# r's stationary operand at 64 columns, u's operands at 64 rows, and the tokens' split issued behind the move of r, in a chunked attention kernel with two MLPs

## The chip, the cores and the metric

The kernel runs on one core of one Trainium2 chip. The metric is the device time in microseconds (us) of one execution. TensorE (PE in the rows; PEld are its weight loads), VectorE (DVE), ScalarE (ACT), GpSimd (POOL) and SyncE (SP, which issues the DMAs) each work through a list of instructions of their own, in the order in which it was written into the program.

## What is computed

Three layers, all in float32. The first is a recurrence over 768 tokens, for 4 batches and 8 heads of width 40; the other two are a SiLU MLP (320 to 2048 and back) and a gated MLP (320 to 1536 and back) over the 3072 rows that come out of it.

```python
for t in range(S):                       # S = 768, state is [B, H, 40, 40]
    y[:, :, t] = einsum('bhd,bhde->bhe', r_t, state)
    Sa = einsum('bhde,bhe->bhd', state, a_t)
    state = state * w_t[:, :, None, :] - outer(Sa, b_t) + outer(v_t, k_t)
x = silu(y_rows @ w_in) @ w_out
x = (sigmoid(x @ w_gate) * (x @ w_val)) @ w_out2
```

## The kernel before

**The recurrence.** The tokens are cut into 24 chunks of C = 32. A unit is one chunk of one batch, and n counts the units, 0 to 95, four batches to a chunk. Inside a unit the 32 tokens are solved at once: a triangular system is inverted on VectorE ahead of time (`z`, `zh`, `zs`), and the unit itself is a row of small float32 matmuls over its 8 heads, each head written as a pair (i, g) with i in 0..1 and g in 0..3. Of a pair of heads one writes the PSUM partitions from 0 on and the other those from 64 on. In the profile each of these matmuls appears as two instructions, a transpose as one. The groups of a unit, by the names of their PSUM tiles:

- `ps_r` (`c_rhs`, L472): the right side of the system, 96 rows deep, from the tokens' tile `xt` (stationary, 32 columns a head) and the state's tile `sr`. ScalarE moves the result to the tile `rb` in two copies (L476). This move of r is what the title speaks of.
- `ps_u` (`c_u`, L486): the inverse, `zs`, times `rb`, 32 rows deep. ScalarE writes the result into `sr` (L488).
- `ps_ut` (L520), `ps_t` (L513), `wt` (L447): transposes. ScalarE moves `wt` to `ks` and `yl` (L450, L451).
- `ps_y` (L543) and `ps_s` (L498): output and new state, both 128 rows deep with 40 columns of weights. VectorE takes them to `stg` (L551) and `sr` (L503).
- `ps_lp` (L529): 64 rows deep, 32 columns of weights, 32 instructions. VectorE takes it to `yr` (L532).
- `lb` (L258): for units that are prepared ahead, 64 rows deep and 64 columns of weights.

All of these but some of the `lb` share one pool of four PSUM buffers (`pt`).

**The order on TensorE.** A loop over n writes the groups out by a string of letters. For n under 16 it is `cuRqz0tp1vys23l`, and the digits are warming matmuls (`acc_w`) that compute nothing. From n = 16 on it is `zcqu0123vtpRysl`; the digits are now a share of the first MLP: 16 matmuls `hp` (L608) and 12 matmuls `acc` (L630 to L632). From there each step reads `ps_lp`, `ps_u`, `hp`, `acc`, `ps_ut`, `ps_t`, `wt`, `ps_r` of the next unit, `ps_y`, `ps_s`. After n = 95 the first MLP goes on alone to n = 111, and then comes the gated MLP.

**Work issued behind other work.** A dictionary `last_q` keeps the last instruction of a unit on ScalarE ("a") and on VectorE ("v"). `behind()` has what is written inside it come after these two in the engines' lists. Three users: the split of the tokens (`x_split`, L589 to L592), which every eighth step makes high and low parts of the recurrence's output for the first MLP; the conversions of the first MLP's weights (`wtick`); and those of the gated MLP's weights (`conv2`). Before the change `last_q["a"]` is the copy of `wt` to `yl` in `prep` (L451), which stands ahead of the move of r on ScalarE. The tool that builds the kernel settles the rest of each engine's order with a timeline of its own, and gives out the PSUM buffers by it.

**Setup.** `setup2` zeroes with ScalarE the parts of the tiles that no DMA fills.

Of the kernel before, what the change touches and what calls it, by code (L numbers as in the profile page):

```python
# [8 lines left out]
F32 = mybir.dt.float32  # L9
# [9 lines left out]
H, D, C, NB = 8, 40, 32, 4  # L19
# [3 lines left out]
KO, WO, EW = 4 * C, 12 * C, 12 * C + GW  # L23
# [10 lines left out]
def kernel(  # L34
# [71 lines left out]
    vu = cp.tile([64, 8, H, C], F32, name="vu")  # L106
    zf = vu[:].rearrange("p a h c -> p (a h c)")[:, 5 * H * C:].rearrange("p (x h c) -> p x h c", x=2, h=H)

    zs2 = [cp.tile([96, 2, 4, C], F32, name=f"zs{i}") for i in range(2)]
    rb = [cp.tile([96, 4, D], F32, name=f"rb{i}") for i in range(2)]  # L110

    etb = [cp.tile([ER, 2, EW], F32, name=f"et{i}") for i in range(NEB)]
    wib = [cp.tile([ER, 2, GW], F32, name=f"wi{i}") for i in range(2)]
# [36 lines left out]
    def setup2(units):  # L150

        for k in units:
            zero(sr[k][32:64])
            if k < 3:
                zero(yl[k][0:64])
            if k < 1:
                zero(ks[k][0:64])
                nc.scalar.copy(ks[k][0:D], ident[0:D, 0:D].unsqueeze(1).to_broadcast([D, H, D]))
            if k < NB:
                zero(sr[k][0:D])  # L160
            if k < NCB:
                zero(yr[k][32:64])
            if k < NXB:
                zero(xt_l(k, 32, 64))
            if k == 0:
                flat = lambda t: t.rearrange("p b h c -> p (b h c)")
                zero(flat(vr2))
                zero(flat(vu[32:64, 0:5]))
                zero(zf)
# [256 lines left out]
            nc.scalar.copy(zs2[n // 2 % 2][64 * i:64 * i + B2, :, :, B2:], ps[:, :, 4 - 4 * i:8 - 4 * i])  # L426

    def xt_a(k, h):
        i, g = divmod(h, 4)
        return xt[k][:, 1 - i, C * g:C * (g + 1)]  # L430

    def xt_l(k, p0, p1):
        return xt[k][p0:p1, :, 0:KO]

    def xt_w(k):
        w = xt[k][0:D, 1, WO:EW].rearrange("p (g s) -> p g s", s=W33)
# [30 lines left out]
    def c_rhs(n):  # L467
        k, s = n % NCB, n % NSB
        ps = pt.tile([128, 4, D], F32, tag="pt", name="ps_r")
        for g in range(4):  # L470
            for i in range(2):
                last_pe[0] = nc.tensor.matmul(  # L472
                    ps[64 * i:64 * i + C, g], xt_a(n % NXB, 4 * i + g), sr[s][0:96, 4 * i + g, :], start=True, stop=True
                )
        for i in range(2):
            nc.scalar.copy(rb[n % 2][64 * i:64 * i + C], ps[64 * i:64 * i + C])  # L476
        rhs_i[n] = last_op[0] = last_pe[0]

    def c_u(n):
# [2 lines left out]
        ps = pt.tile([128, 4, D], F32, tag="pt", name="ps_u")  # L482
        for g in range(4):
            for i in range(2):
                x = slice(64 * i, 64 * i + C)
                last_op[0] = nc.tensor.matmul(ps[x, g], z[x, g], r[x, g], start=True, stop=True)  # L486
        for i in range(2):
            nc.scalar.mul(sr[s][96:128, 4 * i:4 * i + 4], ps[64 * i:64 * i + C], -1.0)  # L488

# [812 lines left out]
```

## Time and profile before

| | us |
|---|---|
| median of 3 runs | 1331.74 |
| lowest, highest run | 1330.07, 1333.38 |
| the profiled execution, its own time | 1330.02 |
| its span, first to last instruction | 1328.3 |
| TensorE busy in the span | 1253.2 (94%) |
| TensorE weight loads busy | 1144.0 (86%) |
| VectorE busy | 762.2 (57%) |
| ScalarE busy | 609.3 (46%) |
| mean granted TensorE clock | 0.972 of 2.4 GHz |

The stages of the span, read from the rows of TensorE: setup to about 54 us, units n = 1 to 15 with warming matmuls to about 215, units 16 to 95 with the first MLP to about 838, the rest of the first MLP to about 911, and the gated MLP to the end. The times of one row are those of one profiled execution. A start of a group minus the start of the group before it is what the earlier group costs the engine, a change between the two included; a matmul's own duration is longer than that, since matmuls overlap.

### The profile page before, as it was taken

The page shows a single profiled execution, that of the slowest core. Times are in us where ns is not written, and L with a number is a line of the kernel's source. Part 1 is how long each engine was busy: PE and PEld are TensorE (multiplying, and loading weights), DVE is VectorE, ACT ScalarE, POOL GpSimd, SP SyncE. Part 2 cuts the span into 40 slices and gives each one's busy share as a digit, 9 for nine tenths or more (in the row PEclk, how much of TensorE's full clock was granted, in tenths as well). Part 3 has the DMA queues.
Part 4 walks back from the last instruction along what each step waited for, and adds up shares of the span by engine and source line. Part 5 has one row for each costly group of instructions (what it writes and reads, how often), then busy time and mean ns, then how long its engine had stood idle before and what let it go on. Part 6 is the DMA issues. An engine that isn't in the chain of part 4 may idle for free. (4 is left out here: it accounts for less than half of the span.)

```text
span 1328.3 us, 44838 instructions
## 1 busy us (share of the span) xinstructions
PE 1253.2 (94%) x18785; PEld 1144.0 (86%) x18785; DVE 762.2 (57%) x2014; ACT 609.3 (46%) x1498; POOL 207.8 (16%) x303
## 2 busy tenths in 40 slices
PE   3788989899999999999999999999999999999996
PEld 3688888899999999989999999988888888888885
DVE  7356775868686777767685733477952323232322
ACT  4236555555555555545555555577532222222221
POOL 3124445311111111111110000133310000000000
PEclk9888887899999999999999999999999999999998
DMA  7666656454545455545544231345610101000000
GB/s 187 143 147 160 187 155 168 138 131 130 130 122 151 117 148 121 142 118 139 133 129 103 70 92 42 91 121 191 186 52 5 35 6 34 7 12 8 12 10 23
DMA packets 167557, 135.98 MB, mean 102 GB/s; under 512 B 89538, under 2 KB 129858, under 8 KB 167346
## 3 DMA queue, kind: packets, MB, share of 16 engines
q1 hardware_dynamic: 167346, 133.02, 38.5%
q8 instruction: 151, 2.47, 0.8%
q14 instruction: 60, 0.49, 0.1%
HBM read 95.15 MB, written 37.48 MB: 100 GB/s over the span
## 5 line engine op out<-in xcount | busy, mean ns | idle before, releaser
L608 PE MATMUL hp<-X,w 120*128 120x256 f32 x1536 | 212.1, 292 | 1.4 <-issue 1.4
L608 PEld LDWEIGHTS hp<-X,w 120*128 120x128 f32 x1536 | 193.9, 194 | 5.7 <-issue 1.5
L1077 DVE TENSOR_TENSOR sg<-hv,sg 128x512 f32<-128x512 f32 x72 | 49.7, 690 | 186.2 <-PE hv L1069 161.5
L1069 PE MATMUL hg<-XT,wgv 128*128 128x512 f32 x576 | 151.2, 394 | 0.5 <-ACT x L639 0.5
L1069 PE MATMUL hv<-XT,wgv 128*128 128x512 f32 x576 | 147.2, 394 | 0.0
L1069 PEld LDWEIGHTS hv<-XT,wgv 128*128 128x128 f32 x576 | 107.3, 188 | 23.5
L1069 PEld LDWEIGHTS hg<-XT,wgv 128*128 128x128 f32 x576 | 105.9, 188 | 21.4 <-ACT x L639 0.8
L630 PE MATMUL acc<-o1h,gh 128*128 128x320 f32 x384 | 119.9, 312 | 2.2 <-ACT gh L618 2.2
L632 PE MATMUL acc<-o1h,gl 128*128 128x320 f32 x384 | 119.4, 311 | 1.8 <-DVE gl L619 1.8
L619 DVE TENSOR_TENSOR gl<-hp,gh 128x512 fp32r<-128x512 f32 x96 | 65.9, 687 | 92.9 <-ACT gh L618 92.6
L631 PE MATMUL acc<-o1l,gh 128*128 128x320 f32 x384 | 119.0, 310 | 0.0
L674 POOL TENSOR_TENSOR cvt<-cvt,cvr 128x256 int32<-128x256 int32 (+3 forms) x85 | 73.3, 868 | 283.4 <-DVE cvt L673 201.6
L551 DVE TENSOR_TENSOR stg<-ps_y,xt 40x128 f32<-40x128 f32 x192 | 55.0, 287 | 105.6 <-PE ps_y L543 102.5
L488 ACT ACTIVATE sr<-ps_u 32x160 f32<-32x160 f32 x192 | 56.4, 294 | 120.0 <-PE ps_u L486 117.8
L617 ACT ACTIVATE hp<-hp 128x512 f32<-128x512 f32 x96 | 55.9, 582 | 121.1 <-PE hp L608 121.1
L341 DVE TENSOR_TENSOR ztmp<-zh,z 128x126 f32<-128x126 f32 (+22 forms) x310 | 97.0, 313 | 7.8 <-DMA z<-sN 1.4
L345 DVE TENSOR_TENSOR zh<-zh,ztmp 128x126 f32<-128x126 f32 (+22 forms) x310 | 97.9, 316 | 6.0
L1078 ACT CAST gh<-sg 128x512 fp32r<-128x512 f32 x72 | 44.6, 620 | 123.6 <-DVE sg L1077 123.4
L1076 ACT ACTIVATE sg<-hg 128x512 f32<-128x512 f32 x72 | 42.9, 596 | 121.6 <-PE hg L1069 121.6
L462 PE MATMUL acc_w<-identr 128*128 128x256 f32 x536 | 87.4, 330 | 1.1 <-issue 1.1
L1089 PE MATMUL a<-o,gh 128*128 128x320 f32 x288 | 87.9, 309 | 0.0
L1088 PE MATMUL a<-o,gh 128*128 128x320 f32 x288 | 87.6, 310 | 0.3 <-ACT gh L1078 0.3
(147 smaller groups left out, 2408.2 us busy)
## 6 DMA issues: line engine op xcount, KB each, us to landing
xt<-sE SPq DMA_DIRECT2D x48, 322.5 KB
sE<-et SPq DMA_DIRECT2D x84, 161.2 KB
et<-in_wkab_dram SPq DMA_DIRECT2D x80, 161.2 KB
cvr<-in_moe_w_out_dram SPq DMA_DIRECT2D x28, 320.0 KB
X<-sX SPq DMA_DIRECT2D x144, 40.0 KB
z<-sN SPq DMA_DIRECT2D x20, 256.0 KB
cvr<-in_moe_w_in_dram SPq DMA_DIRECT2D x42, 100.0 KB
sr<-in_vn_dram SPq DMA_DIRECT2D x48, 80.0 KB
```

Of the source, the lines that this page charges most:

```text
L341: nc.vector.tensor_tensor(tv, z[:, 0:rows, s:s + 1].to_broadcast([128, rows, m]), nt[:, s:s + 1, s + 1:].to_broadcast([128, rows, m]), op= ...
L345: last_inv[0] = nc.vector.tensor_tensor(z[:, 0:rows, s + 1:], z[:, 0:rows, s + 1:], tv, op=ALU.add)
L462: last_op[0] = nc.tensor.matmul(ps[:, :128 * w], identr, identr.unsqueeze(1).to_broadcast([128, w, 128]), start=True, stop=True,)
L608: last_op[0] = nc.tensor.matmul(hp[:, half, :], w1[0:rows, wi_, f * 128:(f + 1) * 128], X[xi][0:rows], start=(pi == 0), stop=(pi == 7),)
L619: nc.vector.tensor_tensor(gl, hp, gh.bitcast(F32), op=ALU.subtract)
L630: nc.tensor.matmul(acc_t[c], a, o1(0, f), start=(f == 0), stop=False)
L631: nc.tensor.matmul(acc_t[c], a, o1(1, f), start=False, stop=False)
L632: last_op[0] = nc.tensor.matmul(acc_t[c], gl[:, fi, 128 * c:128 * c + 128], o1(0, f), start=False, stop=(f == NF1 - 1))
L674: nc.gpsimd.tensor_tensor(ti, ti, lo, op=ALU.add)
L1069: nc.tensor.matmul(hp, wgv[mi][f // 4][0:rows, wi_, f % 4 * 128:f % 4 * 128 + 128], X[0:rows, xi, :], start=(pi == 0), stop=(pi == 7))
L1088: nc.tensor.matmul(acc2_t[t], a, o2[0][f], start=(f == 0), stop=False)
L1089: nc.tensor.matmul(acc2_t[t], a, o2[1][f], start=False, stop=False)
```

## The change

Three edits. (1) `xt_a` hands `ps_r` 64 columns of weights for each head in place of 32, and the matmul writes 64 PSUM partitions in place of 32; the upper 32 are not read. The columns that are read beyond the old ones must be finite, so `setup2` zeroes a further part of `xt`. (2) `rb` and `zs` have 128 partitions in place of 96, their rows 32 to 63 and 96 to 127 are zeroed in setup, and `ps_u` is 64 rows deep in place of 32. (3) `last_q["a"]` is set to the move of r as well, so that whatever `behind()` issues in units from 16 on stands behind it. In units under 16 `prep` is written after `c_rhs` and sets `last_q["a"]` again.

```diff
-    zs2 = [cp.tile([96, 2, 4, C], F32, name=f"zs{i}") for i in range(2)]
-    rb = [cp.tile([96, 4, D], F32, name=f"rb{i}") for i in range(2)]
+    zs2 = [cp.tile([128, 2, 4, C], F32, name=f"zs{i}") for i in range(2)]
+    rb = [cp.tile([128, 4, D], F32, name=f"rb{i}") for i in range(2)]
...
                 zero(xt_l(k, 32, 64))
+                zero(xt_l(k, 64, 96))
+            if k < 2:
+                for p in (32, 96):
+                    zero(rb[k][p:p + 32])
+                    zero(zs2[k][p:p + 32].rearrange("p x g c -> p (x g c)"))
...
     def xt_a(k, h):
         i, g = divmod(h, 4)
-        return xt[k][:, 1 - i, C * g:C * (g + 1)]
+        return xt[k][:, 1 - i, C * g:C * (g + 2)]
 
     def xt_l(k, p0, p1):
-        return xt[k][p0:p1, :, 0:KO]
+        return xt[k][p0:p1, :, (KO if p0 == 64 else 0):KO + C]
...
                 last_pe[0] = nc.tensor.matmul(
-                    ps[64 * i:64 * i + C, g], xt_a(n % NXB, 4 * i + g), sr[s][0:96, 4 * i + g, :], start=True, stop=True
+                    ps[64 * i:64 * i + 64, g], xt_a(n % NXB, 4 * i + g), sr[s][0:96, 4 * i + g, :], start=True, stop=True
                 )
         for i in range(2):
-            nc.scalar.copy(rb[n % 2][64 * i:64 * i + C], ps[64 * i:64 * i + C])
+            last_q["a"] = nc.scalar.copy(rb[n % 2][64 * i:64 * i + C], ps[64 * i:64 * i + C])
...
-                x = slice(64 * i, 64 * i + C)
-                last_op[0] = nc.tensor.matmul(ps[x, g], z[x, g], r[x, g], start=True, stop=True)
+                x = slice(64 * i, 64 * i + 64)
+                last_op[0] = nc.tensor.matmul(ps[64 * i:64 * i + C, g], z[x, g], r[x, g], start=True, stop=True)
```

ScalarE in a step with a split (one of those at n = 23, 31, ... 87 and 95), from the copies of `wt` on; `X` is the tile of the first MLP's input. Before:

```order
L450 COPY ks_188<-wt 64x320
L451 COPY yl_186<-wt 64x320
L589 CAST X<-X 120x512
L590 CAST X<-X 120x256
L476 COPY rb_175<-ps_r 32x160 x2
L488 ACTIVATE sr_184<-ps_u 32x160 x2
L617 ACTIVATE hp<-hp 128x512
```

After:

```order
L456 COPY ks_188<-wt 64x320
L457 COPY yl_186<-wt 64x320
L482 COPY rb_175<-ps_r 32x160 x2
L595 CAST X<-X 120x512
L596 CAST X<-X 120x256
L494 ACTIVATE sr_184<-ps_u 32x160 x2
L623 ACTIVATE hp<-hp 128x512
```

The two casts have moved from ahead of the two copies to `rb` to behind them; nothing else has moved there.

ScalarE in step n = 19, while weights of the first MLP are still being converted (`cvt`, `cvr`, `w`, `o1h` are tiles of that conversion). Before:

```order
L450 COPY ks_188<-wt 64x320
L451 COPY yl_185<-wt 64x320
L670 ACTIVATE cvt<-cvr 128x320
L671 ACTIVATE cvr<-cvr 128x320
L694 CAST w_158<-cvt 120x128 x2
L476 COPY rb_175<-ps_r 32x160 x2
L488 ACTIVATE sr_182<-ps_u 32x160 x2
L703 CAST o1h_3840<-cvt 128x320
```

After:

```order
L456 COPY ks_188<-wt 64x320
L457 COPY yl_185<-wt 64x320
L482 COPY rb_175<-ps_r 32x160 x2
L676 ACTIVATE cvt<-cvr 128x320
L677 ACTIVATE cvr<-cvr 128x320
L700 CAST w_158<-cvt 120x128 x2
L494 ACTIVATE sr_182<-ps_u 32x160 x2
L709 CAST o1h_3854<-cvt 128x320
```

The copies to `rb` have moved ahead of four instructions of the conversion. Steps 17 and 18 show the same exchange.

TensorE at the same place, from `ps_r` to the first matmuls of the first MLP, with the engines that each row waits for. Before:

```order
L472 MATMUL ps_r<-sr_182,xt_165 32x40 [waits PE_49]
L543 MATMUL ps_y<-yr_168,yl_187 40x32 [waits Activation_49]
L498 MATMUL ps_s<-sr_182,ks_188 40x40 [waits Activation_49]
L529 MATMUL ps_lp<-yr_169,vu 32x32 [waits DMAHW2_49,DMAHW4_49,PE_49,Activation_49]
L486 MATMUL ps_u<-rb_175,zs_173 32x40 [waits DVE_49,PE_49,Activation_49]
L486 MATMUL ps_u<-rb_175,zs_173 32x40 [waits Activation_49]
L608 MATMUL hp<-X,w_158 128x256 x16
```

After:

```order
L478 MATMUL ps_r<-sr_182,xt_165 64x40 [waits PE_49]
L549 MATMUL ps_y<-yr_168,yl_187 40x32 [waits Activation_49]
L504 MATMUL ps_s<-sr_182,ks_188 40x40 [waits Activation_49]
L535 MATMUL ps_lp<-yr_169,vu 32x32 [waits DMAHW2_49,DMAHW5_49,PE_49,Activation_49]
L492 MATMUL ps_u<-rb_175,zs_173 32x40 [waits PE_49,Activation_49]
L614 MATMUL hp<-X,w_158 128x256 x16
```

The groups stand in the same order. `ps_r` is 64 wide, and `ps_u` no longer waits for VectorE, since with `rb` copied earlier it is given the PSUM buffer that `ps_r` leaves and not that of `ps_y`. In the steps that hold an `lb` (even n from 20 to 78) `ps_u` waits for VectorE before and after the change alike; at n = 18, which holds one too, it does so only after.

## Rows read from the trace of the kernel before

**Rows 1.** Busy us by stage: stretch, length, engines, granted clock, DMA share, GB/s.

```profile
54.00:215.00 161.00, 145.40 (x2983) 135.28 (x2985) 100.71 (x283) 80.96 (x227) 62.76 (x80) 0.87 0.62 159
262.00:838.00 576.00, 569.98 (x12137) 529.97 (x12134) 387.53 (x1164) 305.64 (x796) 65.06 (x111) 1.00 0.47 117
```

**Rows 2.** Timeline of TensorE, one step without a split: start, us, group, count.

```profile
502.84 0.48 PE L472 MATMUL ps_r<-sr,xt 96*32 96x40 f32 x16
503.25 0.50 PE L543 MATMUL ps_y<-yr,yl 128*40 128x32 f32 x16
503.58 0.50 PE L498 MATMUL ps_s<-sr,ks 128*40 128x40 f32 x16
504.01 0.70 PE L529 MATMUL ps_lp<-yr,vu 64*32 64x32 f32 x32
504.64 0.48 PE L486 MATMUL ps_u<-rb,zs 32*32 32x40 f32 x16
505.04 2.17 PE L608 MATMUL hp<-X,w 120*128 120x256 f32 x16
```

**Rows 3.** Timeline of TensorE, the next step, where an lb stands.

```profile
511.09 1.12 PE L258 MATMUL lb<-et 64*64 64x32 f32 x32
512.14 0.70 PE L529 MATMUL ps_lp<-yr,vu 64*32 64x32 f32 x32
```

**Rows 4.** Weight loads by line: count, busy us, mean ns, idle before.

```profile
L258 PEld LDWEIGHTS lb<-et 64*64 64x64 f32 x1344 | 44.0, 139 | 11.9 <-DVE et L235 9.2
L486 PEld LDWEIGHTS ps_u<-rb,zs 32*32 32x32 f32 x1536 | 36.4, 108 | 15.4 <-ACT rb L476 8.2 <-issue 2.9
L472 PEld LDWEIGHTS ps_r<-sr,xt 96*32 96x32 f32 x1536 | 34.7, 113 | 4.9
```

**Rows 5.** Waits of TensorE from 262 us on: total us, times, longest.

```profile
PE ps_u L486 <- ACT rb L476: 3.6, 10, 0.7
```

**Rows 6.** Timeline of TensorE in a step with a split, n = 55.

```profile
534.46 0.69 PE L529 MATMUL ps_lp<-yr,vu 64*32 64x32 f32 x32
535.47 0.78 PE L486 MATMUL ps_u<-rb,zs 32*32 32x40 f32 x16 [0.32 <-ACT rb L476]
536.18 2.06 PE L608 MATMUL hp<-X,w 120*128 120x256 f32 x15
```

**Rows 7.** Timeline of ScalarE in the same step.

```profile
534.31 0.62 ACT L589 CAST X<-X 120x512 fp32r<-120x512 f32 x1
534.84 0.40 ACT L590 CAST X<-X 120x256 fp32r<-120x256 f32 x1
535.14 0.58 ACT L476 COPY rb<-ps_r 32x160 f32<-32x160 f32 x2
```

**Rows 8.** Timeline of TensorE in steps 17 and 19.

```profile
234.25 0.70 PE L529 MATMUL ps_lp<-yr,vu 64*32 64x32 f32 x32
235.79 0.78 PE L486 MATMUL ps_u<-rb,zs 32*32 32x40 f32 x16 [0.84 <-ACT rb L476]
...
252.20 0.70 PE L529 MATMUL ps_lp<-yr,vu 64*32 64x32 f32 x32
255.12 0.74 PE L486 MATMUL ps_u<-rb,zs 32*32 32x40 f32 x16 [2.23 <-DVE stg L551]
```

**Rows 9.** Busy us in stretches around these steps, columns as in Rows 1.

```profile
236.80:240.10 3.30, 3.30 (x17) 3.30 (x16) 3.13 (x11) 1.16 (x4) 2.18 (x3) 0.50 0.83 240
240.30:253.70 13.40, 12.59 (x296) 11.56 (x294) 11.06 (x35) 9.40 (x28) 3.63 (x6) 1.00 0.53 151
253.90:260.60 6.70, 5.48 (x37) 5.42 (x38) 6.34 (x18) 2.00 (x5) 2.27 (x3) 0.50 0.55 160
```

**Rows 10.** Timeline of TensorE, u of the last unit.

```profile
836.42 0.78 PE L486 MATMUL ps_u<-rb,zs 32*32 32x40 f32 x16 [0.65 <-ACT rb L476]
```

**Rows 11.** ScalarE at the end of setup, and one of its zeroing groups.

```profile
42.17 0.42 ACT L450 COPY ks<-wt 64x320 f32<-64x320 f32 x1 [26.67 <-PE wt L447]
...
L148 ACT ACTIVATE xt<-ident 32x256 f32<-32x256 f32 x6 | 2.4, 404 | 0.0
```

## The prediction

> **What bounds the kernel now.** I read the busy time by stage first. From 262 to 838 us TensorE is busy 569.98 of 576 us at full granted clock, while VectorE is busy 387.53 and ScalarE 305.64 of them [rows 1]. There the order of TensorE's groups is the path: what a group costs the engine is the next start minus its own, and a microsecond taken out of the row comes off the end, since the rest of the first MLP follows on the same engine and the gated MLP's weights are converted behind the last unit of the recurrence. From 54 to 215 us TensorE is busy 145.40 of 161 us, at a mean clock of 0.87, and VectorE and the DMAs hold it up in places [rows 1]; there a change of TensorE's work counts only in part. Then I read one step in order of time [rows 2, 3], the waits that are left in it [rows 5], and the steps in which they fall [rows 6 to 8, 10].
>
> **A change of shape between groups.** `ps_y` and `ps_s` have the same shape of weights and 16 instructions each. From `ps_y` to `ps_s` it takes 503.58 - 503.25 = 0.33 us, from `ps_s` to `ps_lp`, whose weights have another shape, 504.01 - 503.58 = 0.43 [rows 2]. I take 0.10 us as the price of a change of shape. It can be less, since `ps_s` also streams 40 columns and `ps_y` 32: I let it lie between 0.05 and 0.13. The change removes two of these in each step from n = 16 on: from `ps_r` to `ps_y` and from `ps_lp` to `ps_u`. Those before `ps_r` and behind `ps_u` stay, since `wt` and `hp` have other shapes still.
>
> **The wider loads of r.** `ps_r` to `ps_y` takes 503.25 - 502.84 = 0.41 us with a change, so 0.31 without, 19 ns for each of 16 instructions of 32 columns of weights [rows 2]. The trace has 64-column loads in `lb`: 512.14 - 511.09 = 1.05 us with a change behind it, 0.95 without, for 32 instructions [rows 3], so 0.475 for 16. `ps_r` to `ps_y` becomes 0.475 in place of 0.41: +0.065, the change of shape already taken off.
>
> The row of weight loads gives 139 ns for a load of 64 columns and 113 ns for one of 32 [rows 4]; these durations overlap, since a pair for two halves of PSUM runs side by side, and the starts above are what the engine pays. The Trainium skill (TensorE: Matmul & The Clock Gate, "LDWEIGHTS (loading the stationary operand)") has a load take its columns divided by 1.2, in ns, whatever its rows. By that 32 columns more would cost 26.7 ns for each load, an estimate of 0.43 us for 16, and the sum would be nearly that of rival 1. The starts of `lb` disagree.
>
> I go by the starts: 0.475 - 0.31 = 0.165 us for the loads of one `ps_r`.
>
> **The deeper operands of u.** Loads of 32 columns take 108 ns at 32 rows and 113 ns at 96 [rows 4], so 64 rows cost u nothing of note. `ps_lp` to `ps_u` is 504.64 - 504.01 = 0.63 us; without the change of shape 0.53. That is -0.10.
>
> A step gives +0.065 - 0.10 = -0.035 us, and 80 steps (n = 16 to 95) -2.8. With c for the price of a change of shape the step is 0.115 - 1.5 c, so 80 steps give +3.2 at c = 0.05 and -6.4 at 0.13.
>
> **The tokens' split.** Ten times `ps_u` waits for the copies to `rb`, 3.6 us in all [rows 5]. At n = 55 it starts 535.47 - 534.46 = 1.01 us behind `ps_lp` in place of 0.63, and `hp` starts 0.71 behind it in place of 0.40, since its second matmul waits for the second copy [rows 2, 6]. That is 0.38 + 0.31 = 0.69 us. The copies stand behind two casts of the split, which begin at 534.31 [rows 7]. With the casts behind them the copies run from 534.31 to 534.89; `ps_u` would start at 534.46 + 0.065 + 0.53 = 535.05, and the wait is gone with about 0.16 us to spare. What comes late next: the casts run until about 535.7, and the move of u to `sr` behind them. The first MLP's matmuls cover that (`hp` alone lasts 2.17 us [rows 2]) until `ps_ut` reads u, and the split's result is read a step later. Nine steps give 9 x 0.69 = -6.2. The tenth is n = 95, where the idle time is 0.65 and not 0.32 [rows 10], but where fewer groups stand between `ps_r` and `ps_u`; I take -0.8, between -0.3 and -1.1.
>
> **The conversions of the first MLP's weights.** In steps 17 and 19 `ps_u` starts 235.79 - 234.25 = 1.54 and 255.12 - 252.20 = 2.92 us behind `ps_lp` [rows 8], 0.91 and 2.29 more than in a plain step: 3.2 us. The first wait is for `rb`, behind the conversions on ScalarE, which now stand behind it. The second is for VectorE's `stg`, because `ps_u` had been given the buffer that `ps_y` leaves; it no longer is. After both waits the granted clock is 0.50 (1.2 of 2.4 GHz) for 3.3 and for 6.7 us [rows 9]. If it stays up, half of 3.3 and some 2.4 more come back, 4.0 in all. Against that stands VectorE: from 236.8 to 260.6 it is idle for only 0.17 + 2.34 + 0.36 = 2.9 us [rows 9], and `ps_u` of steps 18 and 20 waits for its `stg`. TensorE can gain the 0.9 of step 17 and then about 2.9 before VectorE stops it: 3.8. I take -3.5, with 0 and -7.2 as ends.
>
> **Units 1 to 15.** There the neighbours of `ps_r` are `ps_u` and `ps_lp`, both of other shapes before and after, so nothing is saved, and `ps_r` grows by 0.475 + 0.10 - 0.41 = 0.165 us: 15 x 0.165 = +2.5 if every bit lies on the path, 0 if the 15.6 us in which TensorE idles there [rows 1] take it up. I take +1.2. The order of some DMAs on SP moves there too; I have no row for what that does, and let it be within 2 us either way.
>
> **Setup.** ScalarE gets 14 more zeroing instructions, six more of which have grown. The nearest row has 0.404 us for 256 elements, so at most 5.7 us. ScalarE then waits 26.67 us for TensorE at 42.17 [rows 11], which covers it: 0.
>
> **Sum.** -2.8 - 6.2 - 0.8 - 3.5 + 1.2 = -12.1 us. The profiled execution took 1330.02 us by its own time (span 1328.3), which makes 1317.9; it lies 1.7 below the median of the runs shown, 1331.74, so the median to expect is 1319.6.
>
> **The rivals.**
> 1. The loads of r cost what their records grow by: 139 - 113 = 26 ns for each of 16, 0.416 us and not 0.165, as when the two halves do not load side by side over 96 rows. 80 x 0.25 = +20.1, and +1.9 for units 1 to 15: 1341.6, slower by 0.7%. It decides once `ps_r` to `ps_y` is over some 0.63 us, where the other terms are used up. Against it: the pairs in `ps_y` and `ps_s` do run side by side over 128 rows (0.33 us for 16 loads of 40 columns [rows 2]). Chance 0.06. The Trainium skill's rule for loads, named above, gives nearly the same price for this.
> 2. The change does not do what it says: `ps_r` has 96 rows and `ps_y` 128, and the engine still drains between them and before `ps_u`. Then r grows by 0.165 and u saves nothing: +13.2 for -2.8, 1335.6, 0.29% up and so within what a measurement of this kernel can tell from no change (0.3%). Against it: `lb` changes between 64 and 48 rows inside its own group at 30 ns an instruction [rows 3]. Chance 0.07.
> 3. VectorE takes over in steps 17 to 22, and units 1 to 15 pay in full, with another stretch at half clock: +3.5 + 1.3 gives 1324.4. For it: VectorE is busy 20.5 of the 23.4 us around step 19 [rows 9]. Chance 0.22, of which 0.04 ends within 0.3%.
> 4. The two stretches at half clock go as well: 3.7 us more, 1315.9. Chance 0.07.
>
> **How the numbers follow.** The forecast has 0.58. The other bounds (c, units 1 to 15, the DMAs) move it by some 5 us, the low end is that of rival 4 with these, the high end lies behind rival 3: 1312 to 1327, which leaves out rivals 1 and 2 and a little of the others. Faster by over 0.3% (below 1327.7): 0.58 + 0.07 + 0.18 = 0.83; within 0.3%: 0.07 + 0.04 = 0.11; slower: 0.06.
>
> **What the profile of the changed kernel would show.** From `ps_r` to `ps_y` 0.475 us (0.41 to 0.50; 0.57 speaks for rival 2, over 0.63 for rival 1); from `ps_lp` to `ps_u` 0.53 us; a plain step 0.035 shorter. No wait of `ps_u` for `rb` at n = 23 to 87, and `ps_u` to `hp` 0.40 there. At n = 17 and 19 `ps_u` 0.53 behind `ps_lp`, or at n = 18, 20 or 22 a wait for `stg` in its place. The start of `ps_lp` in step 17 (234.25 us before [rows 8]) shows what setup and the units under 16 did; should it move by more than 3 us, the terms for these were the wrong ones, and the size of the whole is then luck. If the stage from 262 to 838 is not 8 to 11 us shorter, the terms of r, u and the split are wrong.

## The result, and the profile after

| | before | after |
|---|---|---|
| median of 3 runs, us | 1331.74 | 1310.35 |
| lowest, highest run | 1330.07, 1333.38 | 1308.07, 1312.00 |
| the profiled execution, its own time | 1330.02 | 1312.00 |
| its span | 1328.3 | 1310.3 |
| mean granted TensorE clock | 0.972 | 0.980 |

The ratio is 0.9838, 95% interval 0.9807 to 0.9869: 21.4 us faster, where 12.1 were forecast; the time lies 1.7 us under the low end of the range. The direction was right, the size was not. The experiments below also ran the same two kernels again, on other chips, and found less: 13.5, 12.4 and 17.1 us.

A plain step of the changed kernel, the one that answers to [rows 2] (timeline of TensorE; start, us, group, count):

```profile
494.61 0.67 PE L478 MATMUL ps_r<-sr,xt 96*64 96x40 f32 x16
495.09 0.48 PE L549 MATMUL ps_y<-yr,yl 128*40 128x32 f32 x16
495.40 0.48 PE L504 MATMUL ps_s<-sr,ks 128*40 128x40 f32 x16
495.81 0.66 PE L535 MATMUL ps_lp<-yr,vu 64*32 64x32 f32 x29
496.28 0.22 PE L492 MATMUL ps_u<-rb,zs 64*32 64x40 f32 x1
496.28 0.23 PE L535 MATMUL ps_lp<-yr,vu 64*32 64x32 f32 x3
496.34 0.45 PE L492 MATMUL ps_u<-rb,zs 64*32 64x40 f32 x15
496.72 0.86 PE L614 MATMUL hp<-X,w 120*128 120x256 f32 x5
```

From r to y it takes 0.48 us (0.41 before), from lp to u 0.47 (0.63), from r to hp 496.72 - 494.61 = 2.11 in place of 505.04 - 502.84 = 2.20. The first matmul of u now stands ahead of the last three of lp: there is no seam left between the two groups.

A step with a split, n = 55, answers to [rows 6, 7]. The timeline of TensorE, then that of ScalarE:

```profile
525.95 0.66 PE L535 MATMUL ps_lp<-yr,vu 64*32 64x32 f32 x29
526.42 0.22 PE L492 MATMUL ps_u<-rb,zs 64*32 64x40 f32 x1
...
526.85 0.98 PE L614 MATMUL hp<-X,w 120*128 120x256 f32 x6
```

```profile
525.77 0.57 ACT L482 COPY rb<-ps_r 32x160 f32<-32x160 f32 x2
526.37 0.62 ACT L595 CAST X<-X 120x512 fp32r<-120x512 f32 x1
```

The casts begin when the copies to `rb` have ended; u starts 0.47 us behind lp, as in a plain step, and TensorE's `ps_u` no longer waits for `rb` anywhere behind 262 us (ten times before [rows 5]).

The stages as in [rows 1], in the changed kernel (length, busy us of TensorE, its weight loads, VectorE, ScalarE, GpSimd, granted clock, DMA share, GB/s):

```profile
54.00:215.00 161.00, 145.93 (x3018) 136.53 (x3014) 105.92 (x283) 80.83 (x228) 64.36 (x82) 0.89 0.62 158
262.00:838.00 576.00, 573.97 (x12163) 542.19 (x12162) 391.47 (x1170) 313.69 (x813) 68.75 (x118) 1.00 0.47 118
```

Between 262 and 838 us TensorE idles for 2 us where it idled for 6. The stretch is the same in time and not in work: u of the last unit starts at 819.9 us here and at 836.4 before, so the second row takes in some 16 us more of the rest of the first MLP. The first stage has another clock, 0.89 for 0.87; further traces of either kernel, below, scatter as much, so nothing shows that this is the change's doing.

### The profile page after: what moved, and what is told of

Same layout as the page of the kernel before. It is cut to its first block, busy times and chain, and to the rows that moved or that the text cites. A ratio compares the mean times of both kernels' runs of the same rounds, so it can differ in the third digit from the quotient of the medians.

```text
span 1310.3 us, 44861 instructions
## 1 busy us (share of the span) xinstructions
PE 1239.5 (95%) x18785; PEld 1140.2 (87%) x18785; DVE 767.3 (59%) x2014; ACT 613.6 (47%) x1512; POOL 208.9 (16%) x303
## 5 line engine op out<-in xcount | busy, mean ns | idle before, releaser
L1075 PEld LDWEIGHTS hg<-XT,wgv 128*128 128x128 f32 x576 | 105.9, 188 | 21.4 <-ACT x L645 0.8
L625 DVE TENSOR_TENSOR gl<-hp,gh 128x512 fp32r<-128x512 f32 x96 | 65.9, 687 | 77.7 <-ACT gh L624 77.3
L235 POOL TENSOR_TENSOR et<-et 112x256 f32<-112x256 f32 (+1 forms) x42 | 28.2, 671 | 355.8 <-PE hp L614 177.9
```

Source lines behind the costliest of these rows:

```text
L625: nc.vector.tensor_tensor(gl, hp, gh.bitcast(F32), op=ALU.subtract)
L1075: nc.tensor.matmul(hp, wgv[mi][f // 4][0:rows, wi_, f % 4 * 128:f % 4 * 128 + 128], X[0:rows, xi, :], start=(pi == 0), stop=(pi == 7))
```

## The experiments

The theory: the engine pays for a change of shape between two groups, for each column that r loads, and for the wait behind the split, and the three add up; what the result has beyond them is scatter of the first 300 us. The rivals: the parts need each other, or ScalarE, not the shape, sets a step's length, or the change itself shortened the first 300 us. Every step below is the plain step n = 51. The timed comparisons stand against runs of the kernel before on the same chip.

### The three edits apart

a_split_only: the kernel before, and only

```diff
-            nc.scalar.copy(rb[n % 2][64 * i:64 * i + C], ps[64 * i:64 * i + C])
+            last_q["a"] = nc.scalar.copy(rb[n % 2][64 * i:64 * i + C], ps[64 * i:64 * i + C])
```

> The kernel before with one edit: the split of the tokens and the conversions stand behind the move of r on ScalarE; r stays 32 columns wide and u 32 rows high. Own theory (the gain is the sum of three parts that don't touch each other): a plain step as long as in the kernel before (about 7.14 us, lp to u 0.63), no wait of ps_u for rb in steps 23 to 87, u to hp 0.40 there, so 9 x 0.69 + 0.8 = 7.0 us less between the start of u in step 23 and the end, and 0 to 3.5 less from steps 17 to 22: 1321 to 1325. Rival (the copies come early enough only because u's group starts later or r's loads are spread): the waits of ps_u stay at 0.2 us or more in the split steps, under 3 us gained: 1328 to 1331.

Measured: 1319.58 against 1326.21 us, 0.9946 (0.9922 to 0.9970). TensorE in the split step n = 55:

```profile
531.21 0.69 PE L529 MATMUL ps_lp<-yr,vu 64*32 64x32 f32 x32
531.83 0.48 PE L486 MATMUL ps_u<-rb,zs 32*32 32x40 f32 x16
```

A plain step is unchanged, lp to u takes 0.62 us in the split steps too, u to hp 0.41. That is the 0.69 us a split, and the waits are gone with r and u as they were.

a_u_only: rb and zs on 128 partitions with zeros, u 64 rows high, nothing else.

> The kernel before with one edit: u's operands are 64 rows high, zeros below; r 32 columns wide, the order on ScalarE as before. Own theory: lp to u goes from 0.63 to 0.47 us as in the changed kernel and u to hp from 0.40 to 0.44, so 0.12 to 0.16 us less in each of 80 steps, 9 to 11 us in all: 1320 to 1323; the ten waits of ps_u for rb grow by the same 0.1 us each and give one of these back. Rival (the prediction's own price, 0.10 for a change of shape): 0.53 us, 8 x 1 = 8.0 less over 80 steps: 1323.7 and more. Second rival (the shorter step comes from r's edit, by the order in which the two halves arrive): lp to u stays over 0.58, under 4 us gained.

Measured: 1319.80 against 1326.21 us, 0.9941 (0.9916 to 0.9967). TensorE:

```profile
501.68 0.66 PE L533 MATMUL ps_lp<-yr,vu 64*32 64x32 f32 x30
502.18 0.22 PE L490 MATMUL ps_u<-rb,zs 64*32 64x40 f32 x1
...
502.59 0.86 PE L612 MATMUL hp<-X,w 120*128 120x256 f32 x5
```

lp to u 0.50 us, u to hp 0.41: 0.12 us a step, between the two expectations and nearer to the first. In the split steps lp to u stays 1.02 us: there the wait for `rb` takes the gain back.

a_r_only: r 64 columns wide, nothing else.

> The kernel before with one edit: r's stationary operand is 64 columns wide. Own theory: r to y 0.48 us in place of 0.41, y to s and s to lp unchanged or 0.02 less each, lp to u 0.63 as before: a step of +0.03 to +0.07 us, 2 to 6 us more over 80 steps, and the ten waits for rb in the split steps grow by as much less: 1333 to 1338. Rival (the wider r also buys the earlier start of u in step 16, 4.2 us, that the changed kernel shows): u of step 16 starts 3 us or more earlier than in the kernel before, the whole is 1329 to 1333. Against chance: if the second trace of the kernel before has its u of step 16 elsewhere by 3 us as well, this place tells nothing of r.

Measured: 1330.06 against 1326.21 us, 1.0033 (1.0007 to 1.0059): r's edit alone costs time. TensorE:

```profile
500.51 0.67 PE L473 MATMUL ps_r<-sr,xt 96*64 96x40 f32 x16
501.00 0.48 PE L544 MATMUL ps_y<-yr,yl 128*40 128x32 f32 x16
501.30 0.48 PE L499 MATMUL ps_s<-sr,ks 128*40 128x40 f32 x16
501.72 0.70 PE L530 MATMUL ps_lp<-yr,vu 64*32 64x32 f32 x32
```

r to y 0.49 (+0.08), y to s 0.30 and s to lp 0.42 (together 0.04 less): +0.04 a step. The u of step 16 starts at 222.1 us here, 6.8 earlier than in the first trace of the kernel before; further traces, below, show what that is worth.

By time the three edits alone sum to -6.6 - 6.4 + 3.9 = -9.1 us, less than the 12 to 17 us that the whole gives on the chips of the experiments; with intervals of some 3 us either way on each that leaves it open whether they add. In the traces they do: from u of step 24 to u of step 95 the three take 5.6 and 8.3 us less and 1.6 more than the mean of three traces of the kernel before, -12.3 together, and the changed kernel 11.6 less (table below).

b_u_split: the changed kernel with r back at 32 columns.

> The changed kernel with r back at 32 columns: u's operands 64 rows high and the order on ScalarE as changed. The three parts alone gave +0.04 us (r: r to y +0.077, y to s -0.021, s to lp -0.017), -0.11 to -0.16 (u) and no change (split) in a plain step, and 0.7 a split. Own theory (they add): r to y 0.41, lp to u 0.49, u to hp 0.42, a plain step 0.04 us shorter than in the changed kernel, from the start of u in step 25 to that in step 94 2.4 to 3.0 us less than in the changed kernel; total 2 to 5 us below the changed kernel on the same chip, where the stretches at half clock before step 17 can blur it by 4 us either way. Rival (r's 64 columns are needed for u's gain, because the halves of u start apart otherwise): lp to u 0.55 or more, steps no shorter than in the changed kernel.

Measured: 1312.10 us, where the changed kernel takes 1312.72 (below). The step is 0.04 us shorter than in the changed kernel, as expected, but from u of step 25 to u of step 95 it is only 0.5 us less than the mean of four traces of the changed kernel, and the gain of 2 to 5 us did not show: waits for nothing shown (idle time that the profile puts down to "issue"; last section) came to 3.3 us, against 1.1 to 2.2 in those four, with a stretch at half clock behind one of them, as in two of the four. By steps, r's edit is a loss; by time, it can't be told from none.

### What makes the shape

b_u36: the changed kernel, u with 36 columns, so over 32 as in lb, and no longer as lp.

```diff
-                last_op[0] = nc.tensor.matmul(ps[64 * i:64 * i + C, g], z[x, g], r[x, g], start=True, stop=True)
+                last_op[0] = nc.tensor.matmul(ps[64 * i:64 * i + C + 4, g], z[x, C * (4 * (n % 2) + g):C * (4 * (n % 2) + g + 1) + 4], r[x, g], start=True, stop=True)
```

> The changed kernel with 36 columns of weights for u in place of 32, the four more being the next head's, whose products are not read; rows 64 as changed. u then has the shape of lb (64 rows, over 32 columns) and not that of lp. Own theory (u's gain is a change of shape saved): lp to u back at 0.57 to 0.63 us (0.47 in the changed kernel, 0.63 before), a plain step 0.10 to 0.16 longer, 8 to 13 us more over 80 steps. Rival (the gain comes from the rows: 64 rows let the two halves run side by side, whatever the columns): lp to u stays under 0.51, within 3 us of the changed kernel.

Measured: 1316.44 us. TensorE:

```profile
495.45 0.69 PE L538 MATMUL ps_lp<-yr,vu 64*32 64x32 f32 x32
496.08 0.48 PE L495 MATMUL ps_u<-rb,zs 64*36 64x40 f32 x16
496.49 0.50 PE L617 MATMUL hp<-X,w 120*128 120x256 f32 x2
```

lp to u is back at 0.63 us with 64 rows and four more columns. So it is the shape that u's edit saves, not the rows as such. Its price, from r to hp, is 2.24 - 2.11 = 0.13 us.

b_r36: the changed kernel, r with 36 columns in place of 64.

```diff
-        return xt[k][:, 1 - i, C * g:C * (g + 2)]
+        return xt[k][:, 1 - i, C * g:C * (g + 1) + 4]
-                    ps[64 * i:64 * i + 64, g], xt_a(...), ...
+                    ps[64 * i:64 * i + C + 4, g], xt_a(...), ...
```

> The changed kernel with 36 columns of weights for r in place of 64. Own theory (the engine pays for a change between weights of at most 32 and of more than 32 columns, and for each loaded column): r to y 0.30 to 0.34 us (0.49 with 64, 0.41 with 32 columns), y to s and s to lp 0.31 and 0.41 as in the changed kernel, lp to u 0.47: a plain step 0.15 to 0.19 us shorter than in the changed kernel, 12 to 15 us less over 80 steps. Rival (r gains only at exactly 64 columns, as ps_y and ps_s with 40 have a shape of their own): r to y 0.42 or more, within 5 us of the changed kernel. Rival (loads cost the same up to 64 columns): r to y 0.48, the time of the changed kernel.

Measured: 1310.05 us, 2.7 under the changed kernel. TensorE, and ScalarE's copy to ks:

```profile
495.21 0.48 PE L478 MATMUL ps_r<-sr,xt 96*36 96x40 f32 x16
495.52 0.47 PE L549 MATMUL ps_y<-yr,yl 128*40 128x32 f32 x16
495.94 0.51 PE L504 MATMUL ps_s<-sr,ks 128*40 128x40 f32 x16
```

```profile
495.48 0.42 ACT L456 COPY ks<-wt 64x320 f32<-64x320 f32 x1
```

r to y fell to 0.31 us: over 32 columns is enough. But y to s rose to 0.42, and the step is no shorter than with 32 columns. `ps_s` starts at 495.94, when `ks` is ready (495.90). Either ScalarE is late now, or the engine pays for the change in a later group. The remaining runs settle that.

c_r36_ptv: b_r36 with the transposes in another order, so that ks is copied first.

```diff
-            for o in ['cuRqz0tp1vys23l', 'zcqu0123vtpRysl'][n >= NL]:
+            for o in ['cuRqz0tp1vys23l', 'zcqu0123ptvRysl'][n >= NL]:
```

> r at 36 columns as in the run b_r36, with the transposes of the recurrence from n = 16 on in the order wt, ps_t, ps_ut in place of ps_ut, ps_t, wt. In b_r36 r to y fell to 0.31 us, but ps_s then started at 0.04 us behind the end of ScalarE's copy of wt to ks, and y to s grew from 0.31 to 0.42. Own theory (the change of shape is saved there, and a wait of ps_s for ks took its place): with wt first, ScalarE copies ks first, so y to s comes to 0.30 to 0.33 with r to y still 0.31, s to lp 0.41 to 0.44 and lp to u 0.47 to 0.50; a plain step 0.14 to 0.18 us shorter than in the changed kernel, 11 to 14 us over 80 steps, about 1299 to 1303 on the chip on which the changed kernel takes 1312.7. Rival (the engine itself pays a little later for the change that it was spared, whatever ScalarE does): y to s stays at 0.40 or more, within 4 us of b_r36. Rival (another copy is late next, rb for ps_u or vu for ps_lp): s to lp or lp to u grows by 0.1 us.

Measured: 1324.65 us, 2.3 under the kernel before on its chip, where b_r36 had been 16.1 under. y to s stays at 0.40:

```profile
496.63 0.47 PE L549 MATMUL ps_y<-yr,yl 128*40 128x32 f32 x16
497.03 0.51 PE L504 MATMUL ps_s<-sr,ks 128*40 128x40 f32 x16
```

```profile
496.56 0.42 ACT L520 COPY yl<-ps_t 40x320 f32<-40x320 f32 x1
```

`ps_s` starts 0.05 us after the copy of `ps_t` ends (496.98): four PSUM buffers go round, and the copy that frees its buffer is late in this order. The profile names that copy as what ended the wait; `ps_s` does not read its result, so that the reason is the buffer is inferred. This run by itself does not tell ScalarE from the rival. The 14 us between the two are something else: waits of TensorE for nothing shown, 7.4 us against 1.0, and 13.7 us at half clock against none, from u of step 24 to u of step 95 (last section).

c_after_ptv: the same order with r at 64 columns.

> The changed kernel with the order wt, ps_t, ps_ut alone, r at 64 columns. Control for the run above. Own theory: no group of a plain step waits for ScalarE in the changed kernel, so earlier copies of ks buy nothing: r to y 0.49, y to s 0.31, lp to u 0.47, a plain step within 0.03 us of the changed kernel, the time within 3 us of it apart from the first 260 us. Rival (the order itself saves TensorE work): a plain step shorter by 0.05 us or more, 4 us or more gained from n = 25 to 95.

Measured: 1325.01 us. The plain step is the changed kernel's to 0.01 us, as expected of a control; the time is 10.5 us over the changed kernel's on the same chip, by such waits at mostly the same places in the program.

d_r36_early: b_r36 with a second ks, and wt with its copies made a step earlier.

```diff
-        nc.scalar.copy(ks[n % 1][64:128], wt)
+        nc.scalar.copy(ks[n % 2][64:128], wt)
...
-                    prep(n)
+                    for m in (n, n + 1)[:1 + (n >= NL and n + 1 < NS)]:
+                        prep(m)
```

> r at 36 columns as in b_r36, the order of the groups as in the changed kernel, but wt of a unit and its copies to ks and yl are made a step earlier, into a second tile ks. Own theory (the saved change of shape was eaten by a wait of ps_s for ScalarE): r to y 0.31, y to s 0.30 to 0.33, s to lp 0.41 to 0.44, lp to u 0.47 to 0.50 us, a plain step 0.10 to 0.13 us shorter than in b_r36, 7 to 10 us less between u of step 25 and that of step 95 (517.3 in b_r36): 507 to 511. Rival (the engine pays later for the change that it was spared): y to s stays at 0.40 or more, 515 to 519 us for these steps.

Measured: 1314.96 us. TensorE, and ScalarE's copies to rb:

```profile
501.60 0.47 PE L549 MATMUL ps_y<-yr,yl 128*40 128x32 f32 x16
501.90 0.48 PE L504 MATMUL ps_s<-sr,ks 128*40 128x40 f32 x16
502.34 0.70 PE L535 MATMUL ps_lp<-yr,vu 64*32 64x32 f32 x32
502.94 0.48 PE L492 MATMUL ps_u<-rb,zs 64*32 64x40 f32 x16
```

```profile
502.31 0.58 ACT L482 COPY rb<-ps_r 32x160 f32<-32x160 f32 x2
```

y to s came down to 0.30, so `ps_s` had waited for ScalarE. But lp to u is 0.60: `ps_u` starts at 502.94, 0.05 after the second copy to `rb` ends (502.89). The row of copies on ScalarE from `ps_ut` on (vu, yl, ks, yl, rb) has no gap left. The expected 507 to 511 us between u of step 25 and u of step 95 became 524, and only a part of that is ScalarE's: by the steps, each two of them 0.07 us shorter than in b_r36 (517.3 us), it would be some 515. The rest goes with 4.5 us of waits at the places of the last section, where b_r36 had 1.0, and with 10.2 us at half clock, where b_r36 had none.

d_after_early: the same with r at 64 columns.

> The changed kernel with wt, ks and yl made a step earlier, r at 64 columns. Own theory: ps_s does not wait for ks in the changed kernel, so a plain step stays within 0.03 us of it (r to y 0.49, y to s 0.31, s to lp 0.41, lp to u 0.47) and u of step 25 to u of step 95 takes 520 to 523 us. Rival (making wt earlier saves TensorE time by itself): 515 us or less.

Measured: 1319.28 us; the plain step is unchanged to 0.01 us, and u of step 25 to u of step 95 takes 525.1, 2 us over the expectation, with 4 us of waits for nothing shown.

e_r36_early_pool: d_r36_early, with one copy off ScalarE.

```diff
-        last_q["a"] = nc.scalar.copy(yl[n % 3][64:128], wt)
+        if n <= NL:
+            last_q["a"] = nc.scalar.copy(yl[n % 3][64:128], wt)
+        else:
+            nc.gpsimd.tensor_copy(yl[n % 3][64:128], ks[n % 2][64:128])
```

> d_r36_early with the copy of wt to yl taken off ScalarE from n = 17 on: GpSimd copies it from ks. Own theory (ScalarE's row of copies is the next bound): r to y 0.31, y to s 0.30, s to lp 0.44, lp to u 0.47 to 0.50, u to hp 0.41 to 0.44 us, 1.93 to 1.99 from r to hp in place of 2.07 in d_r36_early and 2.12 in the changed kernel; a step 0.12 to 0.18 us shorter than in the changed kernel, 508 to 513 us from u of step 25 to u of step 95 if the waits of TensorE for nothing shown stay within 3 us. Rival (the engine pays for the change later): r to hp stays at 2.04 to 2.08. Rival (GpSimd's copies stand behind its own work): ps_y waits for yl, r to y or the wait ahead of it grows by more than 0.3 us in some steps, 520 us or more.

Measured: 1305.16 against 1326.06 us, 0.9863 (0.9831 to 0.9894), the lowest median of this study; the changed kernel did not run on this chip. TensorE, and GpSimd's copy:

```profile
490.29 0.48 PE L481 MATMUL ps_r<-sr,xt 96*36 96x40 f32 x16
490.60 0.47 PE L552 MATMUL ps_y<-yr,yl 128*40 128x32 f32 x16
490.90 0.48 PE L507 MATMUL ps_s<-sr,ks 128*40 128x40 f32 x16
491.32 0.66 PE L538 MATMUL ps_lp<-yr,vu 64*32 64x32 f32 x30
491.79 0.22 PE L495 MATMUL ps_u<-rb,zs 64*32 64x40 f32 x1
...
492.23 0.39 PE L617 MATMUL hp<-X,w 120*128 120x256 f32 x1
```

```profile
491.10 0.49 POOL L460 COPY yl<-ks 64x320 f32<-64x320 f32 x1 [0.29 <-ACT ks L456]
```

r to hp is 1.94 us, in the expected 1.93 to 1.99. From u of step 25 to u of step 95 it takes 515.8 and not 508 to 513, which allowed 3 us of waits for nothing shown: they come to over 5, and 1.4 more stand at such a place though the profile puts them down to a DMA.

e_r32_early_pool: the same with r at 32 columns.

> e_r36_early_pool with r at 32 columns, so with the change of shape between ps_r and ps_y. Own theory: r to y 0.41, y to s 0.33, s to lp 0.43, lp to u 0.47 to 0.50, u to hp 0.41 to 0.44 us, 2.05 to 2.09 from r to hp, 0.10 more than with 36 columns: 7 to 9 us more between u of step 25 and u of step 95 than e_r36_early_pool, apart from waits for nothing shown. Rival (a change of shape costs nothing, the differences were ScalarE's): r to hp as in e_r36_early_pool to 0.03 us.

Measured: 1319.45 us. TensorE:

```profile
497.47 0.48 PE L481 MATMUL ps_r<-sr,xt 96*32 96x40 f32 x16
499.53 0.38 PE L617 MATMUL hp<-X,w 120*128 120x256 f32 x1
```

r to hp is 2.06, 0.12 more than with 36 columns, and u of step 25 to u of step 95 takes 8.5 us more. That is the price of the change of shape from r to y once nothing hides it, and it rules out the rival that ScalarE made the whole difference. The medians differ by more, 14.3 us; in the two traces 3.9 us of it lie ahead of u of step 25, where traces of one kernel scatter as much.

e_r36_early_dve: VectorE makes the copy, from PSUM.

> The same with VectorE for the copy of wt to yl, from PSUM. Own theory: r to hp 1.93 to 1.99 us where VectorE is free in time; its 0.4 us a step go into the 387 us of 576 in which it is busy; ps_lp, which takes the PSUM buffer of wt, waits for VectorE in steps where that stands in a long operation, so s to lp is 0.44 in some steps and up to 0.8 in others: 512 to 522 us from u of step 25 to u of step 95. Rival (VectorE always has time): as the run on GpSimd.

Measured: 1332.56 us, slower than the kernel before; u of step 25 to u of step 95 takes 536 us, 14 over the expectation. s to lp is 0.72 us in the median step. The waits on TensorE from 262 to 838 us (total us, times, longest):

```profile
PE ps_lp L538 <- ACT rb L485: 10.1, 43, 0.2
PE lb L263 <- issue: 8.4, 30, 0.3
```

I had expected `ps_lp` to wait for VectorE; the profile names ScalarE's copies to rb there, and VectorE's copy to yl for six waits of `ps_u`, 1.9 us in all; `lb` waits for nothing shown. The cause isn't settled.

| r to hp in a plain step, us | r to y | y to s | s to lp | lp to u | u to hp | sum |
|---|---|---|---|---|---|---|
| before | 0.41 | 0.33 | 0.43 | 0.63 | 0.40 | 2.20 |
| a_r_only | 0.49 | 0.30 | 0.42 | 0.62 | 0.41 | 2.24 |
| a_u_only | 0.41 | 0.32 | 0.43 | 0.50 | 0.41 | 2.07 |
| b_u_split | 0.41 | 0.33 | 0.43 | 0.49 | 0.42 | 2.08 |
| after | 0.48 | 0.31 | 0.41 | 0.47 | 0.44 | 2.11 |
| b_r36 | 0.31 | 0.42 | 0.44 | 0.49 | 0.42 | 2.08 |
| d_r36_early | 0.32 | 0.30 | 0.44 | 0.60 | 0.41 | 2.07 |
| e_r36_early_pool | 0.31 | 0.30 | 0.42 | 0.47 | 0.44 | 1.94 |
| e_r32_early_pool | 0.41 | 0.33 | 0.41 | 0.47 | 0.44 | 2.06 |

### The same kernels again

> The kernel before, unchanged, for a second trace. If the stretches at half clock in the units before step 17 fall by chance: they stand at other times or in another number than in the first trace (11 up to 320 us and at 837, 61 us long), the one at 216.3 us may be missing, and u of step 16 starts up to 4 us elsewhere, while a plain step and every split step between 262 and 837 us have the same lengths to 0.02 us. If the change itself took the stretch at 216.3 us away: it is there again, and u of step 16 starts within 1 us of where it did.

> The kernel before once more, for the first 300 us. So far the start of u in step 24 follows the time spent at half clock up to there at about 0.35 us for each us, in traces with and without the change. If that is so, this trace falls on the same line: with x us at half clock before 297 us, u of step 24 starts at 296.8 + 0.35 (x - 57.6), to within 1.5 us. If the change of shape or the split set this length, traces of the kernel before keep 57.6 us of it to within 4.

> The changed kernel, unchanged, for a second trace and for its time on the chip of this comparison. If the start of u in step 16, 4.2 us earlier than before, is chance in the stretches at half clock: it comes elsewhere by 1 to 5 us than in the first trace of the changed kernel, while the steps between 25 and 94 are the same to 0.3 us in sum. If the change did it: u of step 16 starts at 224.7 us to within 1.

> The changed kernel once more. Its first two traces had 41 and 68 us at half clock before 297 us and u of step 24 at 290.1 and 297.0 us. By chance in these stretches it falls anywhere between 288 and 298 us; the part from u of step 24 to u of step 95 is 529 to 530 us (529.8 and 528.5 in the first two, 539.6 in the kernel before), whatever the first part did. If the change fixed the stretches, it starts within 1 us of 290.1.

> The changed kernel once more. Medians on the two chips of the earlier comparisons lay 13.5 and 12.4 us under the kernel before there, the three runs of the result 21.4 under three runs of the kernel before. If the result's excess is chance of three runs each: 11 to 15 us under the kernel before here too. If the change is worth what the result says: 20 us or more.

Measured, with the time at half clock ahead of u of step 24 (61.4 us in the first trace; the 57.6 in an expectation was added up wrongly), and the span cut there and at u of step 95:

| trace | at half clock | start to u 24 | u 24 to u 95 | u 95 to end |
|---|---|---|---|---|
| before | 61.4 | 296.8 | 539.6 | 491.9 |
| a_before_again | 61.4 | 295.9 | 539.5 | 491.5 |
| c_before_again2 | 54.6 | 290.2 | 542.2 | 491.2 |
| after | 41.0 | 290.1 | 529.7 | 490.4 |
| b_after_again | 68.3 | 297.0 | 528.5 | 490.7 |
| c_after_again2 | 44.4 | 288.2 | 527.1 | 490.5 |
| d_after_again3 | 54.6 | 293.3 | 529.8 | 489.2 |

The start of u in step 24 lies anywhere within 7 us in three traces of the one kernel and within 9 in four of the other, so its place in one pair of traces tells nothing of the change. The straight line that I expected against the time at half clock is missed by 4 us in c_before_again2, so the stretches are only part of the scatter. The middle stage, by contrast, holds to some 3 us and is 11.6 us shorter by the means (540.4 to 528.8). With 2.2 in the first part and 1.3 in the last the means differ by 15.1.

| | before on the same chip | changed kernel | difference | ratio |
|---|---|---|---|---|
| the result | 1331.74 | 1310.35 | -21.4 | 0.9838 (0.9807 to 0.9869) |
| b_after_again | 1326.18 | 1312.72 | -13.5 | 0.9902 (0.9872 to 0.9932) |
| c_after_again2 | 1326.92 | 1314.55 | -12.4 | 0.9928 (0.9907 to 0.9948) |
| d_after_again3 | 1327.38 | 1310.24 | -17.1 | 0.9873 (0.9849 to 0.9898) |

The interval of the first meets neither the second nor the third, so the intervals don't cover all that differs between comparisons. Of 118 later runs of the kernel before (median 1326.6, 1319.4 to 1335.8) 16 took 1330 us or more; all three of the result's did. By chance alone three of three would be rare (0.25%, an estimate from 16 of 118), so the chip or the time of the result is the likelier reason; no run settles it. The change is worth about 14 us, the mean of the last three rows.

## Why the prediction was right or wrong, point by point

- **Where the kernel before stands: wrong, and the largest part of the miss.** "The median to expect is 1319.6" leaned on 1331.74, a median of three runs that lies 5.2 us above 118 later ones. From 1326.6 the result is 16.2 us down. Of the 9.3 us between 1319.6 and 1310.35, 5.2 are this; the terms below account for some 2.4, and 1.7 is left to the three runs of the changed kernel. A bound of 2 us on what moves ahead of step 16 was too narrow: u of step 16 starts over 7 to 9 us in traces of one kernel. The warning "the size of the whole is then luck" if it moved by over 3 us applies: the start of `ps_lp` in step 17 moved by 3.2, from 234.25 to 231.01, and in four traces of the changed kernel it lies between 228.9 and 236.5.
- **The price of a change of shape: right mechanism, size too small.** I took c = 0.10 with 0.05 to 0.13 as bounds. b_u36 gives 0.13, e_r32_early_pool against e_r36_early_pool 0.12. In the result lp to u fell by 0.16 where 0.10 was forecast, and u to hp took 0.03 of it back. Part of a change's price stands in the group behind it (y to s 0.33 with a change ahead of it, 0.30 without), which the one difference that I read could not show. The formula 0.115 - 1.5 c gives -0.07 at 0.125; measured was -0.084. Over 80 steps -6.7 in place of -2.8. This is the term of the sum that was mis-sized. With it the stage is shorter than the sum had it: 9.9 us from u of step 24 to u of step 95 in the first pair of traces, inside the 8 to 11 that the prediction named, but 11.6 by the means.
- **The wider loads of r: right.** r to y 0.475 forecast, 0.48 measured. Rival 1 (over 0.63) and rival 2 (0.57, lp to u unchanged) fall. The Trainium skill's rule (TensorE: Matmul & The Clock Gate, "LDWEIGHTS (loading the stationary operand)") would have had 0.43 us, an estimate, for the added columns; r at 64 in place of 36 columns adds 0.48 - 0.31 = 0.17 for 28 columns, where the rule's estimate is 0.37. The measurement decides. What fails is the count of 16 loads: they start in pairs, one for each half of PSUM, 7 ns apart, and from pair to pair it takes 57 ns with 64 columns and 35 with 36. Those 22 ns are near the rule's estimate of 23 for a single load.
- **r's edit as a whole: the right sign.** Forecast was +0.065 a step with the change of shape taken off; alone it is +0.08 between r and y, 0.04 of which comes back in the two groups behind, and 3.9 us slower by time. u and the split carry the gain.
- **The split: right.** 0.69 us each, waits gone, in a_split_only as well.
- **Steps 17 to 22: too large.** Forecast -3.5. From u of step 16 to u of step 24 the three traces of before take 67.9, 67.9 and 68.2 us, the four of after 65.4, 65.9, 65.8 and 69.4. The middle ones differ by 2.1; 0.7 of it is eight shorter steps and 0.7 the split of n = 23, so some 0.7 us is left, with a scatter of 4. The waits of steps 17 and 19 went, as forecast (that of step 17 is missing in c_before_again2 too, so it is not a fixed part of the kernel before); others came, one of them with a stretch at half clock behind it (TensorE at n = 18, then the stretch; columns as above):

```profile
238.16 0.50 PE L549 MATMUL ps_y<-yr,yl 128*40 128x32 f32 x16 [0.69 <-ACT vu L527]
```

```profile
239.45:246.25 6.80, 6.80 (x96) 6.64 (x97) 6.61 (x27) 2.57 (x10) 1.13 (x3) 0.50 0.64 155
```

  That resembles rival 3, though I had named VectorE's stg and the wait is for ScalarE.
- **Units 1 to 15, setup: can't be told** from zero within the scatter. Nor can the 1.3 us behind u of step 95, which the sum did not have.

Together: -12.1, with 3.9 more for the shapes, 2.8 less for steps 17 to 22 and 1.3 more at the end, makes -14.5, beside some 14 us measured.

## What to carry to other kernels

Groups of small matmuls whose weights have one shape run into each other, and a change costs 0.12 to 0.13 us here. What counts as one shape was tried for a few pairs only: 96 rows with 36 or 64 columns and 128 rows with 40 run together, as do two groups of 64 rows with 32 columns; 96 rows with 32 columns against 128 with 40, 32 rows against 64 at 32 columns, and 32 columns against 36 at 64 rows cost the change. Padding buys it off where few columns do it (36 in place of 32), and hardly where loads double (64). Before taking microseconds from the engine that bounds a step, look at the row of copies beside it: ScalarE had 0.1 us to spare and took back the next 0.1 until a copy was moved to GpSimd. And run the kernel before more than three times on more than one chip before a difference of 1% is explained.

## What the runs showed of the hardware that I had not expected

**Waits for nothing shown come at fixed places.** The waits of TensorE from 262 to 838 us that the profile puts down to "issue" grew from 1.9 us in the kernel before to 7.4 and 10.0 in the two with another order of the transposes. They do not come anywhere: counted in records of TensorE (weight loads, matmuls and semaphore instructions, from the start), the waits over 0.25 us in nineteen of the twenty traces, those for rb and vu aside, stand at records 10434, 12482, 13762, 15042, 15810, 17090, 19138, 20418, 22466, 24514, 27842, 29378, 29634 or 31170, to within one, and all of these are a multiple of 256 apart. There are 67 of them, four of which the profile puts down to a DMA. In the twentieth, e_r36_early_dve, thirty waits of 0.28 us ahead of `lb` stand elsewhere; they are not of this kind. Three of the 67, the first at 20418 in b_after_again, the others at 22466 in c_r36_ptv and c_after_ptv:

```profile
540.33 0.25 PE L535 MATMUL ps_lp<-yr,vu 64*32 64x32 f32 x3 [1.09 <-issue]
```

```profile
583.24 0.32 PE L535 MATMUL ps_lp<-yr,vu 64*32 64x32 f32 x5 [2.23 <-issue]
```

```profile
592.11 0.32 PE L535 MATMUL ps_lp<-yr,vu 64*32 64x32 f32 x5 [3.25 <-issue]
```

The page of the profile has a DMA queue for instructions (packets, MB, share of the engines' span):

```profile
q8 instruction: 151, 2.47, 0.8%
```

That is 16.4 KB a packet. The Trainium skill (Runtime: NRT & Kernel Launch, "Instruction fetch mechanics") says that an engine's instructions come in blocks of 256 by a DMA queue of its own, and that crossing a block is mostly hidden; the spacing agrees, and up to 3.25 us are not hidden here. The times of the packets bear it out: each of the 67 waits ends 1.3 to 1.7 us after a packet of 16384 bytes has landed on this queue. In 62 of them TensorE had gone through the 256 records ahead in 4.3 us or less, where the median block of 256 takes 6.4 between 262 and 838 us, so they stand behind blocks that are soon done; most blocks as short have no wait. Why the order of three transposes makes it worse is open: TensorE's list holds 666 semaphore instructions in c_after_ptv and 579 in the changed kernel, so the same groups fall into other blocks, but no run shows that this is the reason.

**Nearly the same idle time drops the clock in one trace and not in another.** In the traces below TensorE had idled for 1.03 and 0.86 us up to 217.06, ahead of the same `wt`; the granted clock of the same stretch behind it is 0.50 in the kernel before and 1.00 in the changed one, 1.2 and 2.4 GHz:

```profile
217.10:226.50 9.40, 9.40 (x79) 8.92 (x80) 5.27 (x13) 5.80 (x15) 5.30 (x6) 0.50 0.71 184
```

```profile
217.10:226.50 9.40, 9.40 (x175) 8.89 (x176) 4.90 (x13) 5.94 (x16) 4.67 (x5) 1.00 0.68 195
```

Traces of one kernel differ as much: ahead of the same `wt`, a_before_again idles for 1.05 us and its half clock starts at 218.8, c_before_again2 idles for 1.95 us and its stretch is 3.4 us long and not 10.2. So the place of a stretch at half clock is nothing to build a term of a sum on.
